# A GpSimd drain in the conditional pairs of a mixture of experts: at the pair's head, or between its two products

## The chip, the cores and the metric

The kernel runs on one core of one Trainium2 chip. The metric is device time in microseconds for one execution of the whole kernel. Beside it stands one profiled execution, whose trace gives every instruction of every engine: TensorE (PE, and PEld for its weight loads), VectorE (DVE), ScalarE (ACT), GpSimd (POOL) and SyncE (SP), which issues the plain transfers. A q behind an engine's name is its sequencer, which hands instructions to the engine and can itself stand at a wait.

## The reference

A small attention block makes 4352 token rows of 512 numbers (8 batches of 512 tokens and 32 states each). A mixture of eight experts follows. Each token goes through one expert, the best by the gate's logits or the expert of the token before it, when a local gate says so:

```python
            if s == 0 or local_gate[b, s] < 0.5:
                e = fresh_e
            else:
                e = prev_e if prev_e >= 0 else fresh_e
            ...
            h = np.maximum(x[b, s] @ w1[e], 0.0)
            out[b, s] = p[e] * (h @ w2[e])
```

w1 is 512 by 1024 and w2 is 1024 by 512 for each expert, all in float32. Which tokens an expert has, and so how many groups of tokens there are, is known only when the kernel runs.

## The kernel before, in words

The attention block comes first, then a routing that gives every token a slot, then the experts. The change touches the experts alone.

The tokens of an expert are cut into *pairs* of two blocks of 128 tokens; what is left over goes into small tiles of 32 tokens. A pair multiplies 256 token rows by w1 (the first product), takes the maximum with zero, and multiplies by w2 (the second product). Each product is made by a scheme of seven smaller matrix products on halves in place of eight (`seven`, called by `strassen` for the first product and by `second_half` for the second), with sums of halves made on VectorE by `add` (line 972).

Pairs 0 to 8 always run and carry a small tile each. Pair 9 always runs too; pairs 10 to 22 stand each inside `tc.If(pairs > u + 1)` of the one before (line 1233), so that only as many run as the routing asked for. These last ones are made by `last`, which calls `pair` with `late=False`. The conditional pairs are the ones meant in the title; pair 9, which `last` also makes, has the same form.

The order of work is written out by hand: an engine carries out its instructions in the order in which the program states them, and waits where an operand isn't there yet. What matters in a pair u:

- **Weights.** SP loads the weights of pair u+1 (`load`, line 915), two quarters at the pair's head and the others at its two calls of `others`.
- **Gathers.** The token rows of a pair come by indirect DMA from GpSimd (`quarter`, line 857), 32 rows' worth of slots at a time: four for each block, eight for a pair. They are paced by `gathers`: ahead of each, GpSimd copies one number of a tile that the pair has just made (the *tick*, line 871), so that the gather isn't issued before that tile is there. The four gathers in the first product of pair u bring the second block of pair u+1; the four in its second product bring the first block of pair u+2.
- **The first product's ticks** read, in turn, the copies s5 and s2 that ScalarE makes of sums in PSUM (line 1078), h11 (line 1062) and s7. The second product's ticks read r5, r2 (line 1100), the low half of the first block's result y, and the whole of it.
- **Transposes.** In the second product, after its first result, `ready(0)` lets VectorE make sums of weights and then `turned(u + 1)`: two transposes (line 885), one for each block of the next pair, which wait for its gathers. The four sums `xs` of `column_sums` follow.
- **Results.** With `late=False`, VectorE then makes the high half of the first block's y (line 1115), adds to the second block's high half, and makes its low half (line 1122). Each block's y goes out by an indirect DMA from GpSimd (`scatter`, line 1038). The first block's scatter is issued inside the second product, ahead of the fourth tick; the second block's is kept in `behind` and issued at the pair's end. Both write the tensor `out`, so a scatter waits until the scatter before it has landed. Last come VectorE's `first_sums(u + 1, 1)`, two sums named a.

A conditional pair loads and gathers for the next pairs even when it turns out to be the last.

`nc.gpsimd.drain()` stands at the head of `last` (line 1229): GpSimd's sequencer holds back what follows it until the engine has finished what was issued. It moves no data, and no other engine is named in it.

Of the kernel before, what the change touches and what calls it, by code (L numbers as in the profile page):

```python
# [138 lines left out]
class Attention:  # L139
# [62 lines left out]
    def bank(self, name, parts=P):  # L202
        return self.ps.tile([parts, 512], F32, name=name)
# [620 lines left out]
def experts(ctx, tc, bank, sums, w1, w2, rows, slots, route, routing, out):  # L824
    nc = tc.nc
# [22 lines left out]
    def places(u, i):  # L848


        n = 7 * u if u == 0 or i else 7 * u - 3
        (w11, w12, w21, w22), sums = [[ring[i][(n + j) % RING] for j in js] for js in (range(4), range(4, 7))]
        return ((w11, w12), (w21, w22)) if i == 0 else ((w11, w21), (w12, w22)), sums
# [12 lines left out]
    def gathers(u, b):  # L866


        for i in range(Q):
            value = yield  # L870
            nc.gpsimd.tensor_copy(tick, value)  # L871
            quarter(xgs_[u % 2][:, b, i], 2 * u + b, i)
        while True:
            yield

    def begun(generator):
        next(generator)
        return generator


    def turned(u):
        for b in range(2):
            to = x_t[:, :, b * P:b * P + P]
            if u:
                nc.vector.transpose(to.rearrange("p k (i t) -> p k i t", i=Q),  # L885
                                    xgs_[u % 2][:, b].rearrange("p i k t -> p k i t"))
                continue

            for h, copy in enumerate((nc.vector.tensor_copy, nc.scalar.copy)):
                t = bank(P, KT * P // 2)  # L890
                for j in range(KT // 2):
                    q = slice((2 * h + j) * P, (2 * h + j + 1) * P)
                    nc.tensor.transpose(t[:, j * P:j * P + P], first[b][:, q], route.ident)
                copy(to[:, 2 * h:2 * h + 2, :], t.rearrange("p (k t) -> p k t", k=KT // 2))
# [5 lines left out]
    def load(u, i, quarters=slice(4)):  # L900

        e = index(slots.experts[0:1, u - 1:u] if u else slots.again if i else slots.expert)
        q = places(u, i)[0]
        for half, other in [((0, 0), (0, 1), (1, 0), (1, 1)), ((0, 0), (1, 0), (0, 1), (1, 1))][i][quarters]:
            to = q[half][other]
            if i:
                w = w2[bass.ds(e, 1), half, :, other]
            else:
                w = w1[bass.ds(e, 1), half, :, other * KT * F // 4:(other + 1) * KT * F // 4]
            if u == 0 and i == 0:  # L910
                chunks = w1[bass.ds(e, 1), half].rearrange("o (q x) (k f) -> (o x) k q f", q=Q, k=KT)
                for j in range(KT):
                    nc.sync.dma_start(out=to[SQ * j:SQ * j + SQ], in_=chunks[:, j, 2 * other:2 * other + 2])
            else:
                nc.sync.dma_start(out=to.rearrange("p k f -> p (k f)"), in_=w.rearrange("o p x -> (o p) x"))
# [55 lines left out]
    def add(out, a, b, op=Alu.add):  # L971
        nc.vector.tensor_tensor(out, a, b, op=op)  # L972
# [12 lines left out]
    def first_sums(u, part):  # L985
        ((a11, a12), (a21, a22)), to = places(u, 0)
        if part == 0:
            add(to[0], a21, a22)
            add(to[1], to[0], a11, Alu.subtract)
        else:  # L990
            add(a21, a11, a21, Alu.subtract)
            add(to[2], a12, to[1], Alu.subtract)

    def column_sums():
        sums_of_rows(xq, (xs[0], xs[1], xs[3]), lambda b22, b12: add(xs[2], b22, b12, Alu.subtract))

    def second_sums(u):
        sums_of_rows(*places(u, 1), lambda b22, b12: add(b12, b12, b22, Alu.subtract))
# [132 lines left out]
    def plain(u, gets):  # L1131

        a = places(u, 0)[0]
        for b in range(2):
            for n in range(2):
                hps = bank()
                for i in range(4):
                    for j in range(KT):
                        nc.tensor.matmul(hps[:, i * P:i * P + P], lhsT=a[n][j // 2][:, j % 2, i * P:i * P + P],
                                         rhs=x_t[:, j, b * P:b * P + P], start=(j == 0), stop=(j == KT - 1))  # L1140
                nc.scalar.activation(hqs[2 * b + n].rearrange("p m t -> p (m t)"), hps, Act.Relu)
                for get in gets:
                    get(hqs[2 * b + n][:, 0, :])
        add(hs[0], c12, h22)
        add(hs[1], hs[0], h11, Alu.subtract)
        add(c12, c12, h11, Alu.subtract)
        add(hs[2], h21, hs[1], Alu.subtract)

    def pair(u, ahead=True, tile=None, after=None, waiting=(), late=True):


        behind = []
        if ahead:
            for i in range(2):
                load(u + 1, i, slice(2) if u or i else slice(4))
        second_sums(u)
        if tile:
            tile.turned()

        def between():  # L1160
            if u == 0:
                next(probabilities)
            if tile:
                tile.one()
            if after:
                after.load(0)
                after.gather()

        def others(i):

            if ahead:
                load(u + 1, i, slice(2, 4))

        def ready(i):
            if ahead:
                first_sums(u + 1, i)
                if i == 0:
                    turned(u + 1)
                    column_sums()

        def getting(v, b):
            if not ahead or v >= NP:
                return lambda value: None
            generator = begun(gathers(v, b))
            return lambda value: generator.send(value[0:1, 0:1])


        gets = [getting(u + 1, 1), getting(u + 2, 0)]
        if u:
            strassen(u, others, gets[0], waiting)  # L1190
        else:
            plain(u, [getting(1, 0), gets[0]])
        between()
        second_half(u, others, ready, gets[1], behind, late)
        if u == 0:
            next(probabilities)
        if tile:
            behind.append(tile.two())
        if after:
            after.load(1)  # L1200
        if not late:
            for results in behind:
                results()
        return behind
# [19 lines left out]
    for u in range(NPMIN - 1):  # L1224
        waiting = pair(u, True, tiles[u], tiles[u + 1] if u + 1 < NTILE else None, waiting)

    def last(u, waiting=()):

        nc.gpsimd.drain()

        pair(u, u + 1 < NP, waiting=waiting, late=False)
        if u + 1 < NP:
            with tc.If(pairs > u + 1):  # L1233
                last(u + 1)

    last(NPMIN - 1, waiting)


# [31 lines left out]
```

## Time and profile before

| | us |
|---|---|
| median of 3 runs (562.53 to 568.31) | 563.67 |
| the profiled execution | 563.83 |
| its span, from first to last instruction | 562.0 |
| PE busy | 529.9 (94%) |
| DVE busy | 375.4 (67%) |
| POOL busy | 309.4 (55%) |
| ACT busy | 168.1 (30%) |
| gathers of token quarters, line 857, 132 of them | 156.8 |
| scatters of blocks, line 1038, 32 of them | 37.6 |

A line of the timeline gives the start from the span's beginning, the duration, engine, source line, operation, and the tile written and read; what stands in brackets is how long the engine had been idle before it and what ended that. A wait is put down to whatever came last by the semaphores; a sequencer that stood at a drain has no semaphore and is not named there. In the list of waits the three numbers are total, count and longest. The drain is the sequencer's own instruction; its line gives the shortest, median and longest duration in nanoseconds, and the first and the last start. POOL's busy share does not hold the drain.

### The profile page before, as it was taken

The page shows a single profiled execution, that of the slowest core. Times are in us where ns is not written, and L with a number is a line of the kernel's source. Part 1 is how long each engine was busy: PE and PEld are TensorE (multiplying, and loading weights), DVE is VectorE, ACT ScalarE, POOL GpSimd, SP SyncE. Part 2 cuts the span into 40 slices and gives each one's busy share as a digit, 9 for nine tenths or more (in the row PEclk, how much of TensorE's full clock was granted, in tenths as well). Part 3 has the DMA queues.
Part 4 walks back from the last instruction along what each step waited for, and adds up shares of the span by engine and source line. Part 5 has one row for each costly group of instructions (what it writes and reads, how often), then busy time and mean ns, then how long its engine had stood idle before and what let it go on. Part 6 is the DMA issues. An engine that isn't in the chain of part 4 may idle for free. (4 is left out here: it accounts for less than half of the span.)

```text
span 562.0 us, 12712 instructions
## 1 busy us (share of the span) xinstructions
PE 529.9 (94%) x4800; PEld 458.3 (82%) x4803; DVE 375.4 (67%) x625; ACT 168.1 (30%) x336; POOL 309.4 (55%) x366
## 2 busy tenths in 40 slices
PE   6889985999999999999999999999999999999991
PEld 2556662698989898988889898989999998999991
DVE  4879988673848474747474757566676584948654
ACT  4656651411222322222323121313232222323220
POOL 6444530165555555555555546462757766677764
PEclk9899997899999999999999999999999999999997
DMA  8999742689998989898989898964757485675742
GB/s 310 417 323 366 265 163 80 183 325 416 371 376 316 356 312 356 311 354 301 365 308 356 309 370 296 382 193 157 249 191 267 148 271 166 227 222 200 266 150 70
DMA packets 50793, 155.44 MB, mean 277 GB/s; under 512 B 9169, under 2 KB 9297, under 8 KB 47394
## 3 DMA queue, kind: packets, MB, share of 16 engines
q1 hardware_dynamic: 43202, 135.85, 66.0%
q0 software_dynamic: 7520, 18.69, 9.9%
q8 instruction: 40, 0.66, 0.5%
q14 instruction: 31, 0.25, 0.1%
HBM read 136.68 MB, written 17.89 MB: 275 GB/s over the span
## 5 line engine op out<-in xcount | busy, mean ns | idle before, releaser
L857 POOL DMA_INDIRECT xg<-rows,row x132 | 156.8, 1188 | 26.0 <-issue 24.8
L972 DVE TENSOR_TENSOR a<-a,a 128x1024 f32<-128x1024 f32 x64 | 76.7, 1219 | 22.6 <-DMA a<-in_w_dram 21.2
L1055 PE MATMUL ps<-xt,a 128*128 128x128 f32 x720 | 88.7, 276 | 0.0
L1055 PE MATMUL sum<-xs,a 128*128 128x128 f32 x720 | 87.8, 275 | 0.0
L1055 PEld LDWEIGHTS ps<-xt,a 128*128 128x128 f32 x720 | 84.4, 192 | 2.1 <-issue 1.8
L1055 PEld LDWEIGHTS sum<-xs,a 128*128 128x128 f32 x720 | 84.0, 192 | 0.0
L972 DVE TENSOR_TENSOR c<-c,c 128x1024 f32<-128x1024 f32 x64 | 75.4, 1219 | 2.9 <-DMA c<-in_w_dram 2.4
L1095 PE MATMUL ps<-c,h 128*128 128x256 f32 x312 | 74.7, 382 | 0.0
L1095 PEld LDWEIGHTS ps<-c,h 128*128 128x128 f32 x312 | 58.1, 190 | 10.9 <-issue 3.7
L1095 PE MATMUL ps<-c,hs 128*128 128x256 f32 x256 | 60.5, 379 | 0.0
L871 POOL COPY tick<-s 1x1 f32<-1x1 f32 x45 | 15.1, 335 | 72.3 <-ACT s L1078 56.1
L1038 POOL DMA_INDIRECT out_dram<-y,tok x32 | 37.6, 1173 | 30.4 <-DVE y L1115 15.7
L1095 PEld LDWEIGHTS ps<-c,hs 128*128 128x128 f32 x256 | 48.7, 190 | 6.6
L885 DVE STREAM_TRANSPOSE xt<-xg 128x512 f32<-128x512 f32 x32 | 21.6, 696 | 42.8 <-DMA xg<-rows,row 42.8
L1095 PE MATMUL sum<-c,h 128*128 128x256 f32 x200 | 47.3, 379 | 0.0
L1095 PEld LDWEIGHTS sum<-c,h 128*128 128x128 f32 x200 | 38.0, 190 | 5.1
L972 DVE TENSOR_TENSOR h<-s,s 128x512 f32<-128x512 f32 x15 | 10.4, 694 | 44.7 <-ACT s L1078 44.7
L482 PE MATMUL v<-sd,a 128*128 128x265 f32 x128 | 35.1, 409 | 4.7 <-DVE a L435 3.2
L1006 ACT COPY sum<-ps 128x256 f32<-128x256 f32 (+1 forms) x31 | 14.3, 460 | 71.0 <-PE ps L1055 49.5
L482 PEld LDWEIGHTS v<-sd,a 128*128 128x128 f32 x128 | 23.0, 195 | 12.0 <-DVE xr L485 3.5
L1100 ACT ACTIVATE r<-sum,prob 128x256 f32<-128x256 f32 x32 | 15.2, 474 | 51.7 <-PE sum L1095 51.7
L1095 PE MATMUL sum<-c,hs 128*128 128x256 f32 x128 | 30.2, 379 | 0.0
(228 smaller groups left out, 736.6 us busy)
## 6 DMA issues: line engine op xcount, KB each, us to landing
c<-in_w_dram SPq DMA_DIRECT2D x68, 512.0 KB, 6.8
a<-in_w_dram SPq DMA_DIRECT2D x64, 512.0 KB, 9.4
at<-in_w_dram SPq DMA_DIRECT2D x18, 1024.0 KB, 8.6
ct<-in_w_dram SPq DMA_DIRECT2D x18, 1024.0 KB, 7.6
x_t<-in_xt_dram SPq DMA_DIRECT2D x16, 512.0 KB, 7.9
x_n<-in_xn_dram SPq DMA_DIRECT2D x8, 1024.0 KB, 9.7
rows<-xr SPq DMA_DIRECT2D x8, 1024.0 KB, 4.3
xg<-rows,row POOLq DMA_INDIRECT x132, 4.2
```

The costliest lines, as they stand in the source:

```text
L482: nc.tensor.matmul(v[:, u, :VW], lhsT=self.a[:, u, c * P:c * P + P], rhs=at.sd[:, b, u * VW:(u + 1) * VW], start=True, stop=True)
L857: nc.gpsimd.indirect_dma_start(out=to.rearrange("p k t -> p (k t)"), out_offset=None, in_=rows.rearrange("n q x -> (n q) x"), in_offset=ba ...
L871: nc.gpsimd.tensor_copy(tick, value)
L885: nc.vector.transpose(to.rearrange("p k (i t) -> p k i t", i=Q), xgs_[u % 2][:, b].rearrange("p i k t -> p k i t"))
L972: nc.vector.tensor_tensor(out, a, b, op=op)
L1006: nc.scalar.copy(y, x)
L1038: nc.gpsimd.indirect_dma_start(out=out, out_offset=to, in_=y, in_offset=None, bounds_check=NT - 1, oob_is_err=False)
L1055: nc.tensor.matmul(to[:, m * P:m * P + P], lhsT=w[:, j, m * P:m * P + P], rhs=x[:, j, :], start=begin and m == 0 and j == 0, stop=(m == FK ...
L1095: nc.tensor.matmul(to, lhsT=x[:, m, :], rhs=w[:, m, :], start=begin and m == 0, stop=(m == FK // 2 - 1), skip_group_check=True)
L1100: nc.scalar.activation(to, t, Act.Copy, scale=p)
```

## The change

The drain leaves the head of `last`. In its place a drain stands in `pair`, after the first product and ahead of the second, for pairs with `late=False`. These are the pairs that `last` makes, so each has one drain as before.

```diff
@@ -1190,6 +1190,8 @@
             strassen(u, others, gets[0], waiting)
         else:
             plain(u, [getting(1, 0), gets[0]])
+        if not late:
+            nc.gpsimd.drain()
         between()
         second_half(u, others, ready, gets[1], behind, late)
         if u == 0:
@@ -1225,8 +1227,6 @@
         waiting = pair(u, True, tiles[u], tiles[u + 1] if u + 1 < NTILE else None, waiting)
 
     def last(u, waiting=()):
-
-        nc.gpsimd.drain()
 
         pair(u, u + 1 < NP, waiting=waiting, late=False)
         if u + 1 < NP:
```

In the programs that the two kernels make, the drain of each such pair stands on GpSimd after the fourth gather of the first product and ahead of the tick on r5, where it stood ahead of the tick on s5. In pair 9 it also comes behind the scatters that the pair before has left over. The instructions of the other engines, their order and their waits are the same. In all pairs that aren't made by `last`, nothing changes.

## The prediction

> **What bounds the kernel now.** I began with the span and TensorE's row in the 40 slices, then cut the stretch that the change touches into its pairs.
>
> ```profile
> span 562.0 us, 12712 instructions
> ...
> PE   6889985999999999999999999999999999999991
> ...
> 501.20:525.80 24.60, 24.60 (x170) 23.16 (x168) 18.06 (x25) 6.42 (x12) 17.36 (x18) 1.00 0.62 215
> 525.80:550.40 24.60, 24.60 (x169) 22.97 (x167) 17.13 (x23) 6.41 (x12) 17.28 (x18) 1.00 0.59 207
> ```
>
> The last two lines are conditional pairs 14 and 15 in the table of stretches (length, then busy time of PE, weight loads, DVE, ACT, POOL). TensorE is busy for all 24.60 us of each. Its timeline is unbroken from 376.25 to 550.55, over all seven conditional pairs. Nothing GpSimd does in them makes TensorE wait, so an edit to GpSimd can win only what follows the last product: 562.0 - 550.55 = 11.45 us.
>
> The second view is the drain's own line: all seven, then the last alone.
>
> ```profile
> L1229 POOLq DRAIN  x7: 3448/4659/12910, 376.0 to 533.5; - x7
> L1229 POOLq DRAIN  x1: 5634/5634/5634, 533.5 to 533.5; - x1
> ```
>
> Seven drains means that pairs 9 to 15 ran. The first is the long one, 12.91 us; the other six take 3.4 to 5.6. The last runs from 533.46 to 539.09.
>
> The third view is who waited for whom after 525.80, and the fourth is the timeline of that last pair.
>
> ```profile
> DVE xt L885 <- DMA xg<-rows,row: 6.1, 1, 6.1
> POOL out_dram L1038 <- DVE y L1115: 4.4, 2, 2.3
> POOL tick L871 <- ACT h L1073: 3.4, 1, 3.4
> ```
>
> ```profile
> 533.86 1.98 POOL L1038 DMA_INDIRECT out_dram<-y,tok  x1 [0.30 <-DVE c L972]
> ...
> 539.23 0.34 POOL L871 COPY tick<-s 1x1 f32<-1x1 f32 x1 [3.39 <-ACT h L1073]
> ...
> 545.10 0.97 POOL L857 DMA_INDIRECT xg<-rows,row  x1 [0.16 <-issue]
> ...
> 548.66 1.89 PE L1095 MATMUL ps<-c,h 128*128 128x256 f32 x8
> ...
> 549.30 0.71 DVE L885 STREAM_TRANSPOSE xt<-xg 128x512 f32<-128x512 f32 x1 [6.09 <-DMA xg<-rows,row]
> ...
> 551.52 0.48 DVE L1115 SCALAR_TENSOR_TENSOR y<-ps,prob,r 128x256 f32<-128x256 f32 x1
> ...
> 552.28 1.01 POOL L1038 DMA_INDIRECT out_dram<-y,tok  x1 [2.27 <-DVE y L1115]
> ...
> 556.50 1.02 POOL L1038 DMA_INDIRECT out_dram<-y,tok  x1 [0.30 <-issue]
> ```
>
> The wait before 539.23 is put down to ScalarE, but that engine had long written the tile (its copy of s began at 529.62): what ended there is the drain. The reader can follow the end from it. The drain holds the four gathers of the first product; the fourth is issued at 545.10, ten microseconds late. VectorE stands 6.09 us for it at its transpose (549.30). In VectorE's queue behind that transpose are the sums xs and the y of line 1115, whose product TensorE had finished at 545.21 + 1.89 = 547.10. The first scatter waits for that y (552.28), then come a tick, a gather and the second scatter (556.50). The chain that ended last shows only this scatter. It lands 2.8 us after its issue, at 559.3, and 2.7 us of closing semaphores and barriers lead to 562.0.
>
> **What the Trainium skill says.** "PSUM — Partial Sum Buffer", section "Engine vs sequencer instructions": a drain waits for its engine to go fully idle. The trace agrees: in six of seven cases it ends 2.2 to 3.3 us after the last DMA instruction on POOL ended (535.84 to 539.09 in the last), about 0.9 us after that DMA's packets had moved. "SBUF — State Buffer", section "Who interferes with whom": a VectorE instruction with two SBUF inputs blocks a GpSimd one that reads SBUF. The trace agrees: a DMA instruction takes 0.97 us alone and 1.93 to 1.98 beside the sums of line 972. "DMA: Bandwidth & Descriptors", section "Anatomy of one DMA — SWDGE (gpsimd) path": a DMA has some 2 us of fixed cost; here 2.8 us from issue to landing for a scatter, measured, which I use.
>
> **The change part by part.** One drain per conditional pair goes from before the pair's first tick to between its fourth and fifth gather. The order of everything else on every engine, each wait and each count of instructions stay as they were. Behind the drain on POOL now stand the ticks and gathers of the second product and both scatters; no longer the first four ticks and gathers. SP's queue is not touched: it issues the weights by its own waits.
>
> *Step 1, taken away at the head.* With no drain, the unconditional pair 8 shows where the four gathers go: its first product starts at 349.40, its first tick at 354.05, its fourth gather at 360.51, so +11.1 us. In pair 15 that is 525.80 + 11.1 = 536.9 instead of 545.10: 8.2 us earlier.
>
> *Step 2, VectorE.* The fourth gather landed 4.2 us after its issue (545.10 to 549.26). Now it lands near 541.1, while VectorE reaches the second transpose at 543.2 (the first one is 542.51 + 0.70). The wait of 6.09 us is gone. Transposes and xs took 2.3 us (549.30 to 551.61), so they end near 545.5, and y of line 1115 now waits for TensorE: 547.10 + 0.1, done at 547.7.
>
> *Step 3, the drain in its new place.* It can end 2.2 to 3.3 us after the fourth gather's instruction (537.9), or, as packets in pair 8 went on until 365.3, 3.8 us after that gather ended, plus 0.9: 540.1 to 542.6. What follows is a tick that needs r5, written at 542.02 + 0.48 = 542.5. So that idle time covers the drain and I cost it at nothing. Without the cover it costs microsecond for microsecond, but only past about 1.5 us: the three ticks and gathers that follow (1.32 us each, as from 546.08 to 547.39, so 4.0) must be done by the 547.95 of step 5, and 542.5 + 1.5 + 4.0 = 548.0.
>
> *Step 4, pair 9.* Its drain, 12.9 us, moves too. Even if it is as long from 390, it ends at 403; the second product's gathers are for the pair after next, and each tile that ScalarE must reuse has a pair's time. Nothing for TensorE: 0.
>
> *Step 5, the tail.* First scatter: y at 547.7 + 0.28 (as 552.00 to 552.28) = 547.95; it lands 2.8 later, 550.75. The second scatter writes the same tensor, so its sequencer waits for that landing; from there to the issue took 0.77 us in pair 9 (411.89 to 412.66): 551.5. Its data: the last product ends at 550.55, line 1122 takes 0.1 + 0.48, then 0.28: 551.4. Both gates agree on 551.5, against 556.50: 5.0 us earlier. But VectorE's two sums a (2.35 us) now start at 551.1, before this scatter and not after the first one, so I take its instruction at 1.98 instead of 1.02: it ends at 553.5, lands 1.78 later at 555.3, and 2.7 more give 557.9. Without the collision it is 557.0.
>
> The profiled execution took 563.83 against its span of 562.0, so 1.83 lies around it: 557.9 + 1.83 = 559.8. The median shown, 563.67, stands 0.16 below that execution: **559.6**. The favourable end is 557.0 + 1.67 = 558.7.
>
> **The rivals.** *No gain:* the last scatter comes no sooner, because VectorE or the first scatter is held by something else, such as a landing of over 5 us (the scatter of 527.58 landed at 532.85, beside VectorE's sums). Both gates would have to move 5 us; the quiet last landing (2.8) speaks against it. About 563.5. *Half:* the drain outlasts r5 by 3 to 4 us; each scatter is some 2 us late: 561.5. *Slower:* the drain right after gathers is long in every pair, as the first was (11.5 us after the last issue). POOL is busy 17.3 us of 24.6 per pair, so the spare is 7.3 us and the drain decides from there. At 11.5 POOL falls 4.2 us behind per pair, 25 over six pairs, of which some 7 us of lead are eaten before TensorE waits for xt, and the 4 us gain are kept: 563.7 + 25 - 7 - 4 = 578. For it: one drain in seven. Against it: six stayed under 3.3, each with as many DMAs since the one before as it will have in the new place.
>
> **How the numbers follow.** Forecast 0.73 (own range 558.5 to 560.6), half 0.10, no gain 0.10, slower 0.07. From 557.9 to 562.7 holds the forecast, half, and little of the rest: 8 in 10. One per cent is what a measurement of this kernel can tell from no change; faster than that needs under 558.03, which is below even the favourable end, so it needs luck of the runs: 0.09. Slower by over 1% is the slow rival: 0.07. The rest, 0.84, is within 1%, on its faster side.
>
> **What would show it.** Right: TensorE unbroken to the last product near 550.5; fourth gather of the last pair near 537 and no wait of VectorE at its transpose; seven drains, the last ending by 543; last scatter near 551.5; a tail of about 7 us after TensorE instead of 11.45. Wrong: drains of over 7 us idle, gaps in TensorE's row, or a last scatter still near 556.

## The result and the profile after

| | before | after |
|---|---|---|
| median of 22 runs each, taken together | 563.6 (558.91 to 570.95) | 558.89 (557.91 to 561.86) |
| the profiled execution | 563.83 | 559.81 |
| its span | 562.0 | 558.0 |
| the tail: from the last product's end to the end of the span | 11.42 | 7.92 |

The ratio is 0.9926, with an interval of 0.9909 to 0.9943; the ratios leave out the executions that lie more than 1.5% above the fastest of their kernel, and before has five such, the change none. The forecast was 559.6, with a range of 557.9 to 562.7 and most of its chance on a gain below one per cent.

The page of after begins as before's did, but TensorE's row ends on a busier slice:

```profile
span 558.0 us, 12712 instructions
PE   6879985999999999999999999999999999999994
```

TensorE again has no gap from pair 9 on. Its last product ends at 550.11 (550.55 before), so this page says what the first view of before let one expect: what changed is the 1 at the end of the row, now a 4, the idle end of TensorE.

The timeline of the last pair (start, duration, engine, line, operation, tiles; in brackets the idle time before it and what ended that) answers line by line to that of before:

```profile
532.07 1.79 POOL L1038 DMA_INDIRECT out_dram<-y,tok  x1 [5.47 <-DVE c L972]
...
539.30 1.25 POOL L857 DMA_INDIRECT xg<-rows,row  x1 [0.16 <-issue]
...
543.86 0.71 DVE L885 STREAM_TRANSPOSE xt<-xg 128x512 f32<-128x512 f32 x1 [1.09 <-issue]
544.38 0.18 POOL L871 COPY tick<-r 1x1 f32<-1x1 f32 x1 [3.83 <-ACT r L1100]
...
546.76 0.48 DVE L1115 SCALAR_TENSOR_TENSOR y<-ps,prob,r 128x256 f32<-128x256 f32 x1 [0.60 <-issue]
...
548.96 1.02 POOL L1038 DMA_INDIRECT out_dram<-y,tok  x1 [0.30 <-issue]
...
550.55 2.35 DVE L972 TENSOR_TENSOR a<-a,a 128x1024 f32<-128x1024 f32 x2
552.80 1.01 POOL L1038 DMA_INDIRECT out_dram<-y,tok  x1 [1.51 <-issue]
```

The fourth gather is issued at 539.30 (545.10 before), VectorE's stand of 6.09 us at its second transpose has become 1.09 (that gather landed at 543.78, just ahead of the transpose), y of line 1115 is made at 546.76 (551.52), and the two scatters go at 548.96 and 552.80 (552.28 and 556.50).

Who waited for whom in that pair, and all seven drains, then the last alone:

```profile
POOL out_dram L1038 <- DVE c L972: 5.5, 1, 5.5
...
POOL tick L871 <- ACT r L1100: 3.8, 1, 3.8
```

```profile
L1194 POOLq DRAIN  x7: 4358/6841/6972, 392.9 to 537.3; - x7
L1194 POOLq DRAIN  x1: 6972/6972/6972, 537.3 to 537.3; - x1
```

The largest wait of before, VectorE for the gathers, no longer leads the list: what is left of it, 1.1 us, stands there under "issue". What leads it now is a scatter on GpSimd, put down to VectorE's c, though what it stood for is the landing of the scatter before it. The 3.8 us of a tick "on ScalarE's r" are the drain, as the 3.39 on h were in before: ScalarE had written that r at 542.06. The drains are longer in their new place, a median of 6.84 us against 4.66.

The saving of 3.94 us of span splits so: TensorE's last pair begins 0.44 earlier, as pair 8 did already (348.96 against 349.40), ahead of any drain of either kernel, so that this isn't the change's doing; the last scatter stands 2.69 us behind the last product and not 5.95, which is 3.26; and from that scatter's issue to the end are 5.24 us and not 5.48, which is 0.24. The change's part in this pair of traces is thus 3.50 us. The medians moved by 4.7; what goes beyond the traces isn't taken apart.

### The profile page after: what moved, and what is told of

Its sections match the earlier page's. It is cut to its first block, busy times and chain, and to the rows that moved or that the text cites. A ratio compares the mean times of both kernels' runs of the same rounds, so it can differ in the third digit from the quotient of the medians.

```text
span 558.0 us, 12712 instructions
## 1 busy us (share of the span) xinstructions
PE 529.5 (95%) x4800; PEld 457.9 (82%) x4803; DVE 377.8 (68%) x625; ACT 168.1 (30%) x336; POOL 287.1 (51%) x366
## 5 line engine op out<-in xcount | busy, mean ns | idle before, releaser
L857 POOL DMA_INDIRECT xg<-rows,row x132 | 148.3, 1124 | 30.6 <-issue 30.1
L1038 POOL DMA_INDIRECT out_dram<-y,tok x32 | 34.5, 1079 | 43.6 <-DVE c L972 27.1
L871 POOL COPY tick<-s 1x1 f32<-1x1 f32 x45 | 16.3, 363 | 49.7 <-ACT s L1078 49.5
L871 POOL COPY tick<-r 1x1 f32<-1x1 f32 x41 | 12.2, 299 | 36.6 <-ACT r L1100 34.3
```

The costliest lines, as they stand in the source:

```text
L857: nc.gpsimd.indirect_dma_start(out=to.rearrange("p k t -> p (k t)"), out_offset=None, in_=rows.rearrange("n q x -> (n q) x"), in_offset=ba ...
L1038: nc.gpsimd.indirect_dma_start(out=out, out_offset=to, in_=y, in_offset=None, bounds_check=NT - 1, oob_is_err=False)
```

## The experiments

*The theories.* The **tail theory** is the prediction's: only the last pair's tail pays, because the drain at its head held four gathers, and with them VectorE and both scatters. One rival says that drains take time in every pair. Another says that GpSimd sets the pace, so that the drains' number decides and TensorE comes to wait. Later runs ask what a drain's length is made of.

**1. No drain at all** (label e1_none).

```diff
-        if not late:
-            nc.gpsimd.drain()
```

> No drain in any pair. Theory of the tail (the drain only matters in the last pair that runs, through the moment at which the last scatter can be issued): in the changed kernel the drain ended 2.2 us after r5 was there, so without any drain the first scatter of the last pair comes about 1.5 us sooner and the time is about 557.3 us. Rival 1 (the drain is hidden where the change puts it): as the changed kernel, 558.9. Rival 2 (the drain does work, such as giving back ring entries, that must then be done elsewhere at a worse moment): a stall of many us on POOL somewhere, 561 or more.

Measured: 567.62, ratio 1.0027 (1.0003 to 1.0052). The scatters did come sooner: the last one at 550.81, 1.77 us behind the last product, where the change has 2.69. Yet the time is that of before, or a little above. The drains that close every program, on GpSimd, show most of the reason:

```profile
L1264 POOLq DRAIN  x3: 40/107/6537, 557.2 to 564.3; - x3
```

One of the three takes 6.54 us; in the change the longest takes 0.65, in before 0.98. The tail is 15.50 us, 7.6 more than the change's: 5.9 of it is this drain, and 2.6 lie between the last scatter's issue and the closing drains (its instruction takes 1.91 us beside VectorE's sums a, not 1.01; the rest is open), less the 0.9 by which that scatter comes sooner. So the scatters went as the tail theory had it, and its time was wrong: work that a drain in the pairs does is otherwise done by the closing drain, with nothing beside it. Run 9 tests that.

**2. The last pair's drain back at its head** (e2_head_in_15). Pairs 9 to 14 stay as in the change.

```diff
-        if not late:
+        if not late and u != 15:
             nc.gpsimd.drain()
...
     def last(u, waiting=()):
+        if u == 15:
+            nc.gpsimd.drain()
```

> The drain between the products in pairs 9 to 14, and at the head in pair 15, which is the last that runs with this data. Theory of the tail: nothing of the gain is left, 562.5 to 563.6 us. Rival (every pair gives its share of the gain, 4.7 / 7 = 0.67 us): six shares stay, 559.6.

Measured: 563.65, ratio 0.9984 (0.996 to 1.0007). No gap on TensorE; the tail is 11.71 us, and the last line of GpSimd is

```profile
556.19 1.02 POOL L1038 DMA_INDIRECT out_dram<-y,tok  x1 [0.30 <-issue]
```

which is 6.20 us behind the last product: before's picture. With six of seven drains moved, the saving is nil. That is the tail theory's value, and the rival of a like share in every pair falls.

**3. Only the last pair's drain moved** (e3_mid_in_15, then once more as e8_mid_in_15_again).

```diff
-        if not late:
+        if u == 15:
             nc.gpsimd.drain()
...
     def last(u, waiting=()):
+        if u != 15:
+            nc.gpsimd.drain()
```

> The drain at the head in pairs 9 to 14, and between the products in pair 15 alone. Theory of the tail: the whole gain, 558.9 us, perhaps up to 1 us more because GpSimd comes late out of pair 14. Rival (every pair its share): one share alone, 562.9.

Measured: 565.24, ratio 0.9997 (0.9967 to 1.0028). The tail theory alone asked for some 559, so this was a miss. The profiled execution, a long one (570.36), has four gaps on TensorE, of 1.14, 1.46, 1.80 and 1.32 us, and its last product ends 5.67 us later than before's. Its tail is no shorter either: 12.37 us. One of them, and the VectorE instructions ahead of it:

```profile
529.91 1.95 PE L1055 MATMUL ps<-xt,a 128*128 128x128 f32 x16
533.18 1.02 PE L1055 MATMUL ps<-xs,a 128*128 128x128 f32 x7 [1.32 <-DVE xs L972]
```

```profile
531.86 0.71 DVE L885 STREAM_TRANSPOSE xt<-xg 128x512 f32<-128x512 f32 x1 [8.78 <-DMA xg<-rows,row]
532.61 0.43 DVE L972 TENSOR_TENSOR xs<-xt 128x256 f32<-128x256 f32 x1
```

The second transpose for a pair is made after that pair has begun on TensorE, and the second of its products needs the sum xs. The gathers come late in pairs 9 to 14, where the drain is at the head. The traces of before and of the change hold the same quantity without a gap. For pair 13, before and then in the change, the first of the four sums xs on VectorE and the product on TensorE that reads it:

```profile
477.41 0.43 DVE L972 TENSOR_TENSOR xs<-xt 128x256 f32<-128x256 f32 x1
478.40 1.95 PE L1055 MATMUL ps<-xs,a 128*128 128x128 f32 x16
```

```profile
470.66 0.42 DVE L972 TENSOR_TENSOR xs<-xt 128x256 f32<-128x256 f32 x1
477.96 1.95 PE L1055 MATMUL ps<-xs,a 128*128 128x128 f32 x16
```

Before, that sum ends at 477.84, 0.56 us ahead of its use; in the change it ends 6.87 us ahead. In pairs 12 to 14 of before the sum is 0.56 to 0.81 us ahead, in pair 15 1.81; in the change it is 6.7 to 7.0 us ahead in all of these. So with the drains at the head TensorE stood within a microsecond of waiting, which no line of a wait list shows.

The second run of this kernel asked for an execution without gaps:

> The drain at the head in pairs 9 to 14 and between the products in pair 15, once more, for its profile. Theory now (the drain at the head makes the next pair's xs late, and TensorE then waits in runs in which the gathers land a little later): if TensorE has gaps at the products with xs they sum to the delay of its last product, and the tail is cut only in so far as GpSimd enters pair 15 on time. Rival (the middle drain of pair 15 alone brings the gain): last scatter within 3 us of the last product.

One run, 559.78, span 558.0, and no gap. The first scatter goes 0.99 us ahead of the last product's end and the last one 3.25 behind it, near the change's 1.15 and 2.69. In an execution that TensorE carries through without a gap, moving the last drain alone brings the last scatter 2.70 us nearer to the last product than before had it (the change: 3.26); in that one execution the tail theory holds for the scatters, though the 3.25 miss the expected 3. The span agrees with the change's only by chance: TensorE ended sooner (548.48), and the last scatter took 6.28 us to the end instead of 5.24, so that the tail is 9.53 us.

Why run 3 shows no gain as a whole stays open. Only one of the 22 executions of e3_mid_in_15 has a trace, and even without executions as long as that one the ratio shows no gain; so gaps of that size don't explain it all. The two traces point to one more thing: GpSimd issued the last scatter of pair 14 11.2 us after pair 15 had begun in the first and 6.8 in the second (before 8.1, the change 6.7). A late GpSimd has the last pair's gathers, and with them both scatters, late as well. If that is so, the drains of the pairs before the last matter too, by where they leave GpSimd. That was not tested apart from the gaps.

**4. A drain in both places** (e4_both). The change, and the head's drain kept.

```diff
     def last(u, waiting=()):
+        nc.gpsimd.drain()
```

> Two drains in each of pairs 9 to 15, at the head and between the products. Theory of the tail: the one at the head holds the first four gathers until about 546, the one in the middle then ends at 549 to 552, three ticks and gathers of 1.32 us follow, and the last scatter is issued 0.5 to 3.5 us later than in the kernel before: 564 to 567 us, 565.5 taken; TensorE still without a gap. Rival 1 (the drain at the head had no cost of its own): 558.9. Rival 2 (GpSimd becomes the bound, since 17 us of work and two idle drains don't fit in 24.6 us): gaps on TensorE and over 570.

Measured: 598.23, ratio 1.0581 (1.0535 to 1.0628), and my figure was 33 us too low. The waits of VectorE for gathers and of TensorE for VectorE's sums, over all conditional pairs:

```profile
DVE xt L885 <- DMA xg<-rows,row: 64.0, 7, 13.3
...
PE ps L1055 <- DVE xs L972: 16.7, 4, 5.5
```

TensorE waits four times, up to 5.5 us, each time for an xs behind a late transpose. The span grew by 31.2 us: these waits are 16.7 of it, the tail 4.7 (16.10 against 11.42), and a later start of pair 10 1.4. Another 8.4 are longer matrix products: around the end of each of the four waits, of 3.5 to 5.5 us, the granted clock of TensorE fell to 0.5, for 3.4 us and the first time for 6.9, and the first 16 products after the first wait took 3.75 us, where they take 1.95. In run 3's trace, with gaps of 1.8 us at most, the clock stayed at 1.00 in these pairs. GpSimd is busy 53% of the span, so its busy time did not set the pace; its two stands in each pair, with the gathers between and behind them, are what this kernel added. This is the prediction's *slower* rival, at another point than the one it gave.

**5. VectorE's transposes ahead of its weight sums** (e5_sums_behind). The question is what a drain waits for. In the change, sums with two inputs run on VectorE while the drain stands; do they hold it?

```diff
             if ahead:
+                if i == 0 and not late:
+                    turned(u + 1)
+                    column_sums()
                 first_sums(u + 1, i)
-                if i == 0:
+                if i == 0 and late:
                     turned(u + 1)
                     column_sums()
```

> The changed kernel, and in the pairs that last makes, VectorE's transposes and sums xs stand ahead of its first two sums a instead of behind them. Theory (the drain between the products is as long as 6.9 us because VectorE's sums a hold up the packets of the fourth gather, which start 0.4 us after those sums end): the drain ends about 2 us sooner, near the moment at which r5 is there, the first scatter of the last pair comes 1 to 1.5 us sooner, and the time is about 1 us under the changed kernel's on the same chip. Rival (the drain's length is its own, whatever VectorE does): drain of 6.9 us as before, time the same as the changed kernel's.

Measured: 562.05, ratio 0.9941 (0.9915 to 0.9967), slower than the change on that chip (559.34 in run 7), though the intervals of the two ratios overlap. The drains take 4.2 to 7.5 us. In pair 14 no such sum ran any more while the last gather's packets were awaited, and the drain still took 7.51, ending 4.22 us after that gather's instruction. So a drain can be as long without those sums beside it. In pairs 10, 11 and 15 it ended 2.4 to 2.9 us after that instruction and not 3.4 to 3.7 as in the change; that the sums had no part in this isn't shown. The loss in time comes from the queue of VectorE: the sums a now stand ahead of the first block's y.

```profile
547.19 2.47 DVE L972 TENSOR_TENSOR a<-a,a 128x1024 f32<-128x1024 f32 x2
...
549.58 0.48 DVE L1115 SCALAR_TENSOR_TENSOR y<-ps,prob,r 128x256 f32<-128x256 f32 x1
```

That y is 2.8 us later than in the change (1.0 of it because TensorE itself ends later, at 551.14), and the first scatter (551.13) and the last follow it. This is once more the tail: 10.28 us.

**6. A drain at the pair's end** (e6_before_kept), ahead of the second block's scatter.

```diff
-        if not late:
-            nc.gpsimd.drain()
         between()
         second_half(u, others, ready, gets[1], behind, late)
...
         if not late:
+            nc.gpsimd.drain()
             for results in behind:
                 results()
```

> One drain per pair made by last, now ahead of the second scatter, at the pair's end, where GpSimd stands anyway until the first scatter has landed. Theory (a drain costs only where something is due behind it): the gathers of both products come as early as without a drain (the first at +8, the fourth at +12 us of the pair), TensorE has no gap, the closing drain stays under 1 us, and the last scatter is issued 2.2 to 4.0 us after the last product against 2.7 in the changed kernel: within 1.5 us of the changed kernel on the same chip, either way. Rival (a drain anywhere ahead of a pair's last scatter costs the tail its whole length): 4 us or more above the changed kernel.

Measured: 559.4, ratio 0.9929 (0.9897 to 0.996), the change's time. In pairs 9 to 14 the drains are the longest of all kernels (8.4 to 9.7 us) and cost nothing, since GpSimd has to stand there for the first scatter's landing anyway: in pair 15 the scatter behind the drain goes at 532.55, and in the change, with no drain there, at 532.07. A drain's length is not its price; what is due behind it is.

**7. The change again on that chip** (e7_change_again).

> The changed kernel once more, beside the others on one chip. Both theories: 558.9 us as first measured, if this chip is like the first; between 0.990 and 0.995 of the kernel before in any case. What is asked is the spread: with the transposes of the next pair done 5.4 us before the pair starts, its runs should lie within 4 us of each other, where those of the kernel before, with about 0.5 us, spread over 12 us and more.

Measured: 559.34, ratio 0.9924 (0.9896 to 0.9951), the first result repeated. In its profiled execution the first scatter goes 1.12 us ahead of the last product's end, as in the first trace, but the last one 4.42 behind it and not 2.69, because the first scatter took longer to land: from its issue to the next one's were 5.5 us and not 3.8. That landing moves the end by nearly two microseconds between executions of one kernel. The spread that was asked for: these 6 runs lie within 1.9 us of each other, the 30 of before on that chip within 8.2, not 12.

**8. The last pair without its weight loads** (e9_no_loads_15). They are for a pair that doesn't run.

```diff
-        if ahead:
+        if ahead and u != 15:
             load(u + 1, 0, slice(0, 2))
...
-            if ahead:
+            if ahead and u != 15:
                 load(u + 1, i, slice(2, 4))
```

> The changed kernel without the loads of weights for pair 16 in pair 15; pair 16 doesn't run with this data, so the outputs keep all their work. Theory (the packets of the fourth gather stand behind a load of weights on the DMA engines: in 20 of the 21 drains that stood behind a full load the packets came some 2 us after the issue, else after 0.6): the drain of pair 15 ends about 2.3 us after its last issue instead of 3.7, the first scatter comes up to 1.3 us sooner after the same product, and the time is 0.5 to 1.3 us under the changed kernel's. Rival (VectorE's sums a, which run until the packets start, hold them up): 3.7 us as before, same time. Here the sums a read weights of an earlier pair and nothing uses their result.

Measured: 560.31, ratio 0.9888 (0.9825 to 0.9951). The last pair's drain, then the transfers of the 7 us around the last gather (538 to 545), first in this kernel, then in the change; the columns are packets, megabytes and the share of the 16 DMA engines:

```profile
L1194 POOLq DRAIN  x1: 3412/3412/3412, 537.3 to 537.3; - x1
```

```profile
DMA packets 55, 0.10 MB, mean 14 GB/s; under 512 B 32, under 2 KB 32, under 8 KB 54
...
q0 software_dynamic: 54, 0.09, 4.3%
```

```profile
DMA packets 234, 0.70 MB, mean 100 GB/s; under 512 B 64, under 2 KB 64, under 8 KB 233
...
q1 hardware_dynamic: 144, 0.52, 22.1%
q0 software_dynamic: 89, 0.17, 7.2%
```

q1 holds SP's weight loads, q0 GpSimd's gathers. Without q1 the drain takes 3.41 us and not 6.97. It ends 2.08 us after the last gather's instruction, in the change 3.68. In both it ends 0.8 us after that gather's packets have moved (539.94 and 543.46). The difference is when those packets come. Over all eleven traces with drains in the pairs, and in place of the count in the expectation: where at least 144 packets of q1 moved between the end of the last DMA instruction and the end of its packets, every drain ended 2.89 us or more after that instruction; where at most 20 did, every one ended within 2.69. The gathers also came 3.2 us sooner within this pair (10.7 us after its start, not 13.9), so this run doesn't separate a shorter drain from an earlier start, and its ratio's interval overlaps the change's.

**9. No drain in the last pair** (e10_none_in_15). Pairs 9 to 14 as in the change.

```diff
-        if not late:
+        if not late and u != 15:
             nc.gpsimd.drain()
```

> The changed kernel with no drain in pair 15. Theory (the closing drain pays for every DMA that GpSimd has issued since the drain before it: 0.23, 0.65 and 0.98 us for 1, 6 and 10 of them, so 0.146 + 0.083 each): with 16 it takes 1.5 us; the last scatter comes 1 us sooner after the last product, as in the kernel without drains (1.8 us); together the same time as the changed kernel or 0.5 us less. Rival (a drain left out makes the end wait for something of a fixed size): a closing drain of 6.5 us as in the kernel without drains, 5 us above the changed kernel.

Measured: 561.23, ratio 0.9925 (0.9898 to 0.9951), the change's ratio. Again the scatters come sooner (the last 1.35 us behind the last product), and again the closing drain is longer:

```profile
L1266 POOLq DRAIN  x3: 46/107/1466, 555.7 to 557.8; - x3
```

This settles the closing drain's price. In run 6 one DMA of GpSimd had been issued since the last drain, in the change six, in before ten, here sixteen; the longest closing drain took 0.24, 0.65, 0.98 and 1.47 us. That is 0.146 us plus 0.083 for each. The other traces with six or ten lie within 0.01 us of these values, but for run 4 (six, 0.54). By that line the 6.54 us of run 1 are 77 DMAs, of 184 that it issued; what became of the rest isn't shown. A fixed price for a missing drain is excluded.

## Why the prediction was right, by its steps

**What bounds the kernel: right for the trace, too strong as a sentence.** The gain is in what follows the last product, as run 2 shows. But "Nothing GpSimd does in them makes TensorE wait" was read from an unbroken row. The row was unbroken by less than a microsecond in three pairs, and run 3's trace, with the same head drains in pairs 9 to 14, has the gaps. What I missed is the slack of an operand, not a wait. The change widens it to nearly 7 us. That fits with its runs lying closer together (within 4 us; before's within 12). On the other chips before's runs spread over 8 to 20 us and run 3's over 13, while the kernels with no head drain in pairs 9 to 14 (runs 1, 2 and 5 to 9, with 6 to 22 executions each) stay within 6. But no long execution of before has a trace, so this second benefit is argued, not shown.

**Step 1, the fourth gather: late by 2.8 us.** It gave +11.1 us into the pair, measured were +13.9. (By that step the drain made it 8.2 us late, not the "ten microseconds" of the reading before it.) I took pair 8, which has no conditional pair before it. In pair 15 GpSimd first stands 5.47 us at the second scatter of pair 14, the first line of the timeline above: it waits for the first scatter's landing, which took some 7 us beside the pair's weight loads. Before, the same scatter went at 533.86, 8.1 us into the pair, and I put the whole lateness of the fourth gather on the drain that stood there too.

**Step 2, VectorE's wait: right in effect.** Of 6.09 us 1.09 are left, not nothing, because the late gather landed at 543.78 and not near 541.1. But the sums xs then end at 546.16, VectorE idles 0.60 us more ahead of y, and y is done at 547.24, against 547.7 less the 0.44 of the earlier start.

**Step 3, the drain's cover: failed by 2.2 us.** "So that idle time covers the drain and I cost it at nothing": r5 was there at 542.06, the drain ended at 544.23. Two things added up: the late gather of step 1, and 3.68 us from its instruction to the drain's end. As an interval this lies inside the step's 2.2 to 4.7, but the start had moved. The page "Perfetto Trace Analysis" of the Trainium skill, section "DMA Instruction — SWDGE (GPSIMD)", says that such an instruction's recorded end is the end of descriptor making and not of the transfer; the trace agrees, the packets ended 2.9 us later. "DMA: Bandwidth & Descriptors", section "Queues, rings and completion order", says that a DMA engine takes turns between its queues, a packet at a time, and that a packet typically holds some 9 to 17 descriptors. What the trace lists as packets did not alternate one by one: 104 of the load's 144 had begun before the first of the gather's 32 did. The 144 are nine for each of 16 engines, so they may be the page's descriptors, and the load one turn; that is a reading, not shown. Run 8 shows the load's removal, with the reservation made there. The first scatter was therefore 1.45 us late against 547.51 (548.96). The three ticks and gathers behind the drain took 4.3 us, about the 4.0 of the step. Here the *half* rival came partly true.

**Step 4, pair 9: right in price, wrong in kind.** Its drain takes 4.36 us in the new place, not 12.9. Nothing waited for it.

**Step 5, the tail: the sum right through errors that cancel.** The last scatter was expected at 551.06 (551.5 less 0.44) and came at 552.80, 1.74 late: 1.45 from step 3, the rest a landing of 3.1 us instead of 2.8. The collision with VectorE's sums didn't come, because the scatter came as they ended (they run from 550.55 to 552.90): 1.01 us instead of 1.98. The closing drain had fewer DMAs to finish. From the issue to the end were 5.24 us against the 6.4 of the step. So 1.74 - 0.44 - 1.16 = +0.14: span 558.04 against 557.9 (the step's own figures add up to 557.96). That the sum came out is luck: steps 1 and 3 were short by more than two microseconds each, and what made up for it (an earlier start that no drain caused, the collision that stayed out and a quicker end) is no part of those steps.

**The rivals.** *No gain* fell: both gates moved. *Slower* fell for this change: with one drain in each pair TensorE has no gap; with two, in run 4, it has.

**The last link.** The chain of waits of after ends as step 5 has it, with a gather and a stand before the last scatter:

```profile
550.29 1.00 POOL xg L857
551.29 1.29 issue
552.58 0.06 POOLq L1233
552.63 0.17 issue
552.80 1.01 POOL out_dram L1038
```

The 1.29 of "issue" are the first scatter's landing (552.01) and the sequencer's way from it. No view names a landing that a sequencer waits for; it has to be put together from the transfers.

## What to carry to other kernels

Price a drain by what is due behind it in its queue, not by its length: 9 us cost nothing where the queue had to stand anyway, and taking 5.6 us from a pair's head, for 7.0 between its products, brought the last scatter 3.3 nearer to the last product. An unbroken row of the bounding engine is no proof of safety; measure how far ahead of its use each operand is ready, since 0.6 us and 7 us of slack look the same in a list of waits. Before a wait or a drain is taken away, look where its work goes then: here the closing drain took it back.

## What the runs showed of the hardware

- A GpSimd drain in a pair ends 0.5 to 1.1 us after the packets of the last DMA before it have moved, in all traces but for the first drain of the kernels that have it at the head in pair 9. So it waits for the transfers as well: that DMA's own instruction on the engine had ended 1.6 to 7.1 us before the drain did. The first drain of those kernels ends 5.1 us after the packets (four traces), as if much was left to finish.
- The closing drain costs 0.146 us plus 0.083 us for each DMA that GpSimd issued since its last drain, within 0.01 us over 1 to 16 DMAs in ten traces; run 4 lies 0.1 below that, and run 1, with no drain before, far below.
- In the kernels whose first drain comes later, GpSimd stands 3.07 us before one gather of pair 9, its 114th DMA (387.45 in the change, and the same DMA in runs 2 and 5 to 9); run 1, which has no drain, shows 2.59 there. Together with the point before it looks like finished transfers being cleared up, at a drain or when a store of them is full. That was not tried and stays open.
- Around the end of a stand of 3.5 to 5.5 us TensorE's granted clock fell to 0.5, for 3.4 us and once for 6.9 (run 4); after gaps of up to 1.8 us it stayed at 1.00 (run 3).
- From the first scatter of the last pair to the second, which waits for its landing, were 3.8 us in one execution of the change and 5.5 in the other. Why is open too.
- No run beat the change clearly: with the drain at the pair's end, without it in the last pair, or without the last loads, the intervals overlap.
